# A top-k attention and MLP kernel: the mask from the k-th score minus the scores, weights decoded through PSUM, and a planner that takes transposes in turn

## The chip, the cores and the metric

The kernel runs on 1 core of one Trainium2 chip. The metric is the device time of one launch in microseconds (us), the median over repeated runs; lower is better. Engines are named as in the profile: PE (TensorE matmul, PEld its weight loads), DVE (VectorE), ACT (ScalarE), POOL (GpSimd), SP (SyncE, which here issues the DMAs).

## The reference

Top-k attention over 4 batches, 8 heads, 576 positions and head size 64, then two MLPs on the 2304 tokens of width 512 with a hidden width of 2048. The weights arrive as float64 and are read as pairs of 32-bit words.

```python
scores = (1 / sqrt(64)) * q @ k.T                    # per head, 576 x 576
kth    = np.partition(scores, -32)[..., -32:-31]     # 32nd largest of each row
scores = np.where(scores >= kth, scores, -1e9)
attn   = softmax(scores)
x      = (attn @ v)  as tokens x 512
h = x @ w_in;   g = h if h >= 1, 0 if h <= -1, else (h + 1)**2 / 4;   x = g @ w_out
h = max(x @ w_in2, 0);   out = (h * h) @ w_out2
```

## The kernel before

**Work.** A slot is one 128-row score tile of one head: 144 slots, eight to a token tile T. For each slot PE writes 576 scores into a PSUM area (there are two areas, used in turn). DVE then finds the 32 largest of each row with four MAX8 and three MATCH_REPLACE8, which take the first scores from PSUM and go on in an SBUF tile W. POOL makes two one-column numbers from the maxima (`exp_bias`, tile nb), ACT masks with a Prelu that reads the scores once more (`below`) and so is the last reader of the PSUM area, ACT takes the exponential (`exp`), ACT and POOL split it into a high and a low half (tile pc), SP issues a DMA transpose (pT), and PE multiplies by v (`attend`). Every token tile then has four groups in each MLP: 12 matmuls into a tile h, ACT and DVE work on it (`mlp_act`, `mlp_gate`), a split on ACT and POOL (tile g), a DMA transpose (gT), and 12 matmuls into o.

**Weights.** All four weight matrices end in one SBUF tile, wall. A chunk (64 of them, two of them in halves) is loaded as float64 words, decoded to fp32 by `w_decode` on ACT, POOL and DVE, measured on PE (`w_norm`, tiles gram), and once its whole matrix is decoded scaled and split into two fp16 halves (`w_split`; for 24 chunks the low half goes PE to ACT through PSUM tiles lo_i and lo_o). The decodes run during about the first 230 us, among the first slots.

**Order.** `Book.order` is a planner: it gives each operation a cost (`Book.costs`), a key (its step, eight steps to a slot, less a shift for urgent kinds) and its dependencies, and runs all five engines' lists forward in planned time. The order that comes out is the order in which each engine's queue is written; on the chip an engine works through its queue in order and waits on semaphores. The planner keeps operations of different engines apart that hold the same "bank": a PSUM tile, or "port", which every POOL operation holds and every DVE operation with two SBUF inputs.

**Buffers.** PSUM pool `ps_h` has two buffers under one tag "h", given out in rotation: the h tiles of the MLP groups, the lo tiles of `w_split` and the small tiles of `global_scale` share it. An allocation waits until the last but one has been released. The maxima (m8) have three buffers, nb and W four each.

```python
        if engine == "POOL" or engine == "DVE" and sum(not v.tile.ring.psum for v in ins if v.elements() > 64) > 1:
            op.banks.add("port")
    ...
    dch=(0, 1, 3)          # steps of the three parts of a decode
    scores=-6, bias=7, below=8, exp=9, phi=10
```

Of the kernel before, what the change touches and what calls it, by code (L numbers as in the profile page):

```python
# [8 lines left out]
F32 = mybir.dt.float32  # L9
# [7 lines left out]
P = 128  # L17
# [130 lines left out]
class Book:  # L148
# [36 lines left out]
    def note(self, engine, method, fn, args, kwargs):  # L185
        op = Op()
        op.n, op.engine, op.fn, op.args, op.kwargs = len(self.ops), engine, fn, args, kwargs
        views = [a for a in (*args, *kwargs.values()) if isinstance(a, View)]
        outs = [a for a in (*args[:1], kwargs.get("out"), kwargs.get("accum_out")) if isinstance(a, View)]
        ins = [a for a in views if not any(a is o for o in outs)]  # L190
        if method == "matmul" and not kwargs["start"]:
            ins.append(args[0])
        deps = set(self.hold)
        op.tiles, op.new = [], []
        for v in views:
            t = v.tile
            if t not in op.tiles:
                op.tiles.append(t)
                t.left += 1
                if t.first is None:  # L200
                    t.first = op.n
                    op.new.append(t)
                else:
                    deps.add(t.first)
        for v in ins:
            c = v.cover()
            before = [n for d, n in v.tile.writes if meet(c, d)]
            assert before, (method, v.tile.name)
            deps.update(before)
            v.tile.reads.append((c, op.n))  # L210
        for v in outs:
            c = v.cover()
            t = v.tile
            for kind in (t.writes, t.reads):
                kept = []
                for d, n in kind:
                    if n == op.n:
                        kept.append((d, n))
                        continue
                    if meet(c, d):  # L220
                        deps.add(n)
                        if not c[4] and c[0] <= d[0] and c[1] >= d[1] and c[2] <= d[2] and c[3] >= d[3]:
                            continue
                    kept.append((d, n))
                kind[:] = kept
            t.writes.append((c, op.n))

        op.opens = op.closes = []
        if method == "matmul":
            p0, p1, at = outs[0].cover()[:3]  # L230
            parts = [(outs[0].tile, at // 2048, p) for p in range(p0 // 64, (p1 + 63) // 64)]
            op.opens = parts if kwargs["start"] else []
            op.closes = parts if kwargs["stop"] else []
        op.load = method == "dma_start"
        op.move = method
        if op.load:
            if self.beat:
                deps.add(self.beat[-1])
        elif len(self.beat) > WINDOW:
            deps.add(self.beat[-WINDOW])  # L240
        if engine == "DVE" and method == "max":
            self.beat.append(op.n)
        deps.discard(op.n)
        op.deps = deps
        op.banks = {v.tile for v in views if v.tile.ring.psum}
        if engine == "POOL" or engine == "DVE" and sum(not v.tile.ring.psum for v in ins if v.elements() > 64) > 1:
            op.banks.add("port")
        op.cost = self.costs(engine, method, args, kwargs, outs, ins)
        op.key = (self.step + self.shift, op.n)
        self.ops.append(op)  # L250


    def costs(self, engine, method, args, kwargs, outs, ins):
# [7 lines left out]
        if method == "dma_start_transpose":  # L261
            return (1.33 if n < 1100 else 1.41), n * 256 / 1000 / 165
        if method == "dma_start":
            return 0.6, 4 * (n or args[1].elements()) * 128 / 1000 / 400
        if engine == "DVE":
            if method == "max":
                return 0.68, 0.75
# [7 lines left out]
        if method == "memset":  # L275
            return 0.07, 0.07
        c = 0.14 + n / 522 if method == "tensor_tensor" else 0.14 + n / 940 + (0.08 * aps if n < 8 else 0.0)
        return c, c


    def order(self):
# [35 lines left out]
        while len(out) < len(ops):  # L317
# [29 lines left out]
            if op.closes:  # L347
# [1 line left out]
                for s in shut:  # L349
                    heapq.heappush(soon[s.engine], (t, s.n))  # L350
                shut.clear()
            for b in op.banks:
                held.setdefault(b, {})[e] = t + took + 0.08
            free[e] = t + busy
            if op.load:
                wire = max(wire, t + 1.6) + took
                end = wire + 0.7
            elif op.move == "dma_start_transpose":
                wire = max(wire, t + 1.1) + took
                end = wire + 0.4  # L360
            else:
                end = t + took
            out.append(op)
            for n in op.succ:
                s = ops[n]
# [30 lines left out]
def tile_topk_attention_mlp_mlp(  # L396
# [111 lines left out]
    def w_decode(name, c, *half):  # L508
        d = wall[:, W[name]["at"] + c + 1, :].bitcast(I32)
        if half:  # L510
            d = d[:, 256 * half[0] : 256 * half[0] + 256]
        words = lambda: raw[(name, c, *half)].rearrange("p (n w) -> p n w", w=2)
        halves = lambda: raw[(name, c, *half)].bitcast(U16).rearrange("p (n w) -> p n w", w=4)
        hi = lambda: words()[:, :, 1]


        low = lambda: halves()[:, :, 1]
        return [
            lambda: ACT.activation(hi(), hi(), AF.Prelu, scale=2.0**-112, alpha=-(2.0**32)),
            lambda: POOL.tensor_scalar(d, low(), 2.0**-13, 2.0**-14 - 0.5, op0=ALU.mult, op1=ALU.add),  # L520
            lambda: DVE.scalar_tensor_tensor(d, hi().bitcast(I32), 3, d, op0=ALU.logical_shift_left, op1=ALU.bitwise_or),
        ]

    gram = {}
# [252 lines left out]
    def q_scale(T):  # L777
        n2 = small.tile([P, 1], F32, tag="qn2", name=f"qn2_{T}")
        sq = small.tile([P, 2], F32, tag="sq", name=f"sq_{T}")
        esc = small.tile([P, 2], F32, tag="esc", name=f"esc_{T}", bufs=3)  # L780

        ld["sq", T] = sq

# [7 lines left out]
        def exp_scale():  # L791
            for half in range(2):
# [1 line left out]
                POOL.tensor_scalar(  # L794
                    esc[:, half : half + 1], isk[:, b : b + 1], sq[:, 1:2], 0.125, op0=ALU.mult, op1=ALU.mult
                )
            POOL.tensor_scalar(esc, esc, 2.0**-56, 1.0, op0=ALU.max, op1=ALU.mult)
            ld["esc", T] = esc

        return (  # L800
# [6 lines left out]
    def q_prep(T, half):  # L807
# [21 lines left out]
        def trans():  # L829
# [2 lines left out]
                out=qt.rearrange("p a h t -> p (a h) t"), in_=hl().rearrange("p a h b d -> p (a h b d)")  # L832
            )
            for jj in range(4):
                st[8 * T + 4 * half + jj] = dict(qt=qt[:, :, jj, :], esc=ld["esc", T][:, half : half + 1])

        return [split_hi, split_lo, copy_lo, trans]

# [38 lines left out]

    def exp_bias(t):
        d = st[t]
        nb = small.tile([P, 2], F32, tag="nb", name=f"nb_{t}", bufs=4)  # L880
        last = d["m"][:, TOPK - 1 : TOPK]
        d["nb"] = nb
        if t in PLAN["md"]:
            POOL.tensor_scalar(nb[:, 1:2], d["m"][:, 0:1], d["esc"], -1.0, op0=ALU.mult, op1=ALU.mult)
            return
        POOL.tensor_scalar(nb[:, 0:1], last, -1.0, 1.0, op0=ALU.mult, op1=ALU.mult)
        POOL.tensor_scalar(nb[:, 1:2], last, d["m"][:, 0:1], d["esc"], op0=ALU.subtract, op1=ALU.mult)

    def below(t):
        d = st[t]  # L890
        if t in PLAN["md"]:
            return
        ACT.activation(d["e"], d["s"], AF.Prelu, bias=d["nb"][:, 0:1], scale=1.0, alpha=2.0**97)

    def exp(t):
        d = st[t]
        by = t in PLAN["md"]
        ACT.activation(d["e"], d["s"] if by else d["e"], AF.Exp, bias=d["nb"][:, 1:2], scale=d["esc"])
        if by:
            DVE.scalar_tensor_tensor(d["e"], d["s"], d["m"][:, TOPK - 1 : TOPK], d["e"], op0=ALU.is_ge, op1=ALU.mult)  # L900

# [510 lines left out]
```

## Time and profile before

| | us |
|---|---|
| median of 3 runs (lowest, highest) | 1121.82 (1120.46, 1122.23) |
| profiled execution, its own time | 1122.3 |
| its span in the profile | 1120.4 |
| PE busy in the span | 986.2 (88%) |
| DVE busy | 918.2 (82%) |
| ACT busy | 868.2 (77%) |
| POOL busy | 719.0 (64%) |

The span is what the trace covers; 1.9 us of the execution's own time lie outside it. A busy share is a mean over stages: in the first quarter of the span weights are loaded and decoded among the first slots, the middle holds slots and MLP groups, and the last 110 us or so hold MLP groups alone.

### The profile page before, as it was taken

The page shows a single profiled execution, that of the slowest core. Times are in us where ns is not written, and L with a number is a line of the kernel's source. Part 1 is how long each engine was busy: PE and PEld are TensorE (multiplying, and loading weights), DVE is VectorE, ACT ScalarE, POOL GpSimd, SP SyncE. Part 2 cuts the span into 40 slices and gives each one's busy share as a digit, 9 for nine tenths or more (in the row PEclk, how much of TensorE's full clock was granted, in tenths as well). Part 3 has the DMA queues.
Part 4 walks back from the last instruction along what each step waited for, and adds up shares of the span by engine and source line. Part 5 has one row for each costly group of instructions (what it writes and reads, how often), then busy time and mean ns, then how long its engine had stood idle before and what let it go on. Part 6 is the DMA issues. An engine that isn't in the chain of part 4 may idle for free.

```text
span 1120.4 us, 20689 instructions
## 1 busy us (share of the span) xinstructions
PE 986.2 (88%) x6676; PEld 478.3 (43%) x6676; DVE 918.2 (82%) x1992; ACT 868.2 (77%) x1605; POOL 719.0 (64%) x1182
## 2 busy tenths in 40 slices
PE   1258577777999999999999999999999999999997
PEld 0034333333444444454444444444444444444443
DVE  3988888798999999999899999999899999992100
ACT  4568879998987777888888888988788778776532
POOL 4596989979786756557776646567685646454221
PEclk9999888789999999999999999999999999999999
DMA  7996887686897766878988687879867676654332
GB/s 205 305 311 177 239 230 160 139 178 116 145 168 147 132 117 118 157 133 155 170 145 147 109 128 128 159 136 172 156 123 129 114 133 99 120 109 99 71 61 56
DMA packets 463389, 165.21 MB, mean 147 GB/s; under 512 B 441777, under 2 KB 448945, under 8 KB 463281
## 3 DMA queue, kind: packets, MB, share of 16 engines
q1 hardware_dynamic: 459856, 163.05, 71.5%
q10 hardware_dynamic: 3424, 0.85, 0.5%
q8 instruction: 52, 0.85, 0.3%
q14 instruction: 57, 0.46, 0.1%
HBM read 55.31 MB, written 4.72 MB: 54 GB/s over the span
## 4 chain that ended last, share of the span: by engine, by line
PE 31%; POOL 15%; issue 10%; ACT 9%; DMA 9%; DVE 9%; SPq 1%; POOLq 0%; ACTq 0%; DVEq 0%
PE o L383 14%; PE h L383 12%; DMA gT<-g 5%; POOL pc L383 4%; DVE m L383 4%; PE s L383 4%; DVE W L383 3%; POOL g L383 3%; POOL wall L383 3%; ACT r L383 2%; ACT W L383 2%; POOL nb L383 2%; SPq L383 1%; DMA l_q<-in_q_dram 1%; ACT g L383 1%
## 5 line engine op out<-in xcount | busy, mean ns | idle before, releaser
L383 PE MATMUL o<-wall,gT 128*128 128x512 f16 x1728 | 427.7, 383 | 18.6 <-DMA gT<-g 17.1
L383 DVE MAX8 m<-W 128x8 f32<-128x576 f32 x432 | 326.0, 756 | 7.1
L383 POOL TENSOR_TENSOR g<-r,g 128x512 f16<-128x512 f32 x144 | 167.0, 1160 | 173.0 <-ACT g L383 157.6
L383 PEld LDWEIGHTS <-gT 128*128 128x128 f16 x1728 | 164.1, 98 | 226.6 <-DMA gT<-g 41.8
L383 POOL TENSOR_TENSOR pc<-W,pc 128x64 f16<-128x64 f32 (+1 forms) x288 | 208.9, 745 | 68.3 <-ACT pc L383 63.7
L383 DVE MATCH_REPLACE8 W<-m,W 128x576 f32<-128x576 f32 x288 | 213.8, 743 | 0.0
L383 PE MATMUL h<-wall,T_x 128*128 128x512 f16 x864 | 209.7, 384 | 1.7 <-DVE r L383 1.1
L383 PE MATMUL h<-wall,T_y 128*128 128x512 f16 x864 | 207.3, 379 | 0.2 <-ACT r L383 0.2
L383 ACT ACTIVATE W<-s,nb 128x576 f32<-128x576 f32 x144 | 106.0, 736 | 46.4 <-POOL nb L383 39.8
L383 DVE MAX8 m<-s 128x8 f32<-128x576 f32 x144 | 109.5, 760 | 37.9 <-PE s L383 25.8
L383 PE MATMUL s<-kst,qT 128*128 128x64 f16 (+3 forms) x640 | 102.0, 300 | 35.9 <-ACT W L383 33.0
L383 ACT ACTIVATE W<-W,nb,esc 128x576 f32<-128x576 f32 x144 | 124.6, 865 | 11.1 <-POOL nb L383 5.1
L383 PEld LDWEIGHTS <-T_x 128*128 128x128 f16 x864 | 81.6, 99 | 94.4 <-issue 7.8
L383 PEld LDWEIGHTS <-T_y 128*128 128x128 f16 x864 | 81.3, 98 | 91.2 <-issue 0.7
L383 PEld LDWEIGHTS <-pT 128*128 128x128 f16 (+1 forms) x2240 | 90.8, 102 | 60.8 <-issue 17.6
L383 PE MATMUL s<-vst,pT 128*128 128x65 f16 (+1 forms) x2240 | 98.9, 196 | 13.9 <-DMA pT<-pc 9.5
L383 DVE MATCH_REPLACE8 W<-m,s 128x576 f32<-128x576 f32 x144 | 107.6, 748 | 0.0
L383 ACT ACTIVATE pc<-W 128x576 f16<-128x576 f32 x144 | 97.3, 676 | 1.2
L383 ACT ACTIVATE g<-r 128x512 f16<-128x512 f32 x144 | 89.8, 624 | 8.8 <-DVE r L383 7.4
L383 ACT ACTIVATE r<-r 128x512 f32<-128x512 f32 x144 | 90.5, 629 | 2.8
L383 ACT ACTIVATE r<-h 128x512 f32<-128x512 f32 x72 | 42.5, 590 | 62.7 <-PE h L383 61.3
L383 ACT ACTIVATE r<-h,B,A 128x512 f32<-128x512 f32 x72 | 55.8, 775 | 42.1 <-PE h L383 41.3
(143 smaller groups left out, 1101.0 us busy)
## 6 DMA issues: line engine op xcount, KB each, us to landing
wall<-in_moe_w_in_dram SPq DMA_DIRECT2D x32, 512.0 KB, 7.6
wall<-in_moe_w_out_dram SPq DMA_DIRECT2D x30, 512.0 KB, 5.3
out_dram<-ob SPq DMA_DIRECT2D x18, 256.0 KB, 2.6
l_q<-in_q_dram SPq DMA_DIRECT2D x16, 256.0 KB, 3.5
n_v<-in_v_dram SPq DMA_DIRECT2D x24, 144.0 KB, 2.8
n_k<-in_k_dram SPq DMA_DIRECT2D x12, 288.0 KB, 3.2
l_k<-in_k_dram SPq DMA_DIRECT2D x12, 288.0 KB, 3.3
pT<-pc SPq DMA_TRANSPOSE x144, 3.4
```

The source lines that it names most:

```text
L383: op.fn(*(real(a) for a in op.args), **{k: real(a) for k, a in op.kwargs.items()})
```

## The change

It has three parts. **Mask**: `below` computes Prelu(kth - s), with the 32nd maximum itself as its bias and a scale of -1; a slope of 2^-97 on the side of the kept scores is taken back by `exp`, whose scale is now -(2^97) times the old one (two more columns of tile esc, clamped so that the product stays finite, made by one more POOL operation per token tile). `exp_bias` is left with one POOL operation instead of two. **Decode**: the three parts of a decode come in the order POOL, ACT, DVE instead of ACT, POOL, DVE; ACT writes the decoded high words to a tile of the "h" ring in PSUM instead of back over the raw words in SBUF, the planner lets that operation start only behind the POOL part, and the DVE operation takes one input from PSUM, so that it no longer holds the "port" bank. **Planner**: DMA transposes hold a bank "turn", which keeps those of SP's queue and of ACT's queue apart until the data have landed; a plain load costs 0.1 us more on the wire and counts at half the rate where its target has three or more dimensions; a POOL operation that reads 16-bit words costs 0.1 us more.

```diff
@@ note
+        if method == "dma_start_transpose":
+            op.banks.add("turn")
@@ costs
         if method == "dma_start":
-            return 0.6, 4 * (n or args[1].elements()) * 128 / 1000 / 400
+            n = n or args[1].elements()
+            return 0.6, 0.1 + 4 * n * 128 / 1000 / (200 if outs and len(outs[0].ap.ap) > 2 else 400)
...
+        if any(v.ap.dtype is U16 for v in ins):
+            c += 0.1
         return c, c
@@ order
-            for b in op.banks:
-                held.setdefault(b, {})[e] = t + took + 0.08
...
+            for b in op.banks:
+                held.setdefault(b, {})[e] = end + 0.08
@@ w_decode
         low = lambda: halves()[:, :, 1]
+        ps = []
+
+        def bits():
+            POOL.tensor_scalar(d, low(), 2.0**-13, 2.0**-14 - 0.5, op0=ALU.mult, op1=ALU.add)
+            ps.append(len(book.ops) - 1)
+
+        def top():
+            ps.append(ps_h.tile([P, 4, P], F32, tag="h", name=f"dec_{name}_{c}").rearrange("p a b -> p (a b)")[:, 0 : 256 if half else 512])
+            book.hold = ps[:1]
+            ACT.activation(ps[1], hi(), AF.Prelu, scale=2.0**-112, alpha=-(2.0**32))
+            book.hold = ()
+
         return [
-            lambda: ACT.activation(hi(), hi(), AF.Prelu, scale=2.0**-112, alpha=-(2.0**32)),
-            lambda: POOL.tensor_scalar(d, low(), 2.0**-13, 2.0**-14 - 0.5, op0=ALU.mult, op1=ALU.add),
-            lambda: DVE.scalar_tensor_tensor(d, hi().bitcast(I32), 3, d, op0=ALU.logical_shift_left, op1=ALU.bitwise_or),
+            bits,
+            top,
+            lambda: DVE.scalar_tensor_tensor(d, ps[1].bitcast(I32), 3, d, op0=ALU.logical_shift_left, op1=ALU.bitwise_or),
         ]
@@ q_scale
-            POOL.tensor_scalar(esc, esc, 2.0**-56, 1.0, op0=ALU.max, op1=ALU.mult)
+            POOL.tensor_scalar(esc[:, 0:2], esc[:, 0:2], 2.0**30, 2.0**-56, op0=ALU.min, op1=ALU.max)
+            POOL.tensor_scalar(esc[:, 2:4], esc[:, 0:2], -(2.0**97), 1.0, op0=ALU.mult, op1=ALU.mult)
@@ exp_bias
-        POOL.tensor_scalar(nb[:, 0:1], last, -1.0, 1.0, op0=ALU.mult, op1=ALU.mult)
-        POOL.tensor_scalar(nb[:, 1:2], last, d["m"][:, 0:1], d["esc"], op0=ALU.subtract, op1=ALU.mult)
+        POOL.tensor_scalar(nb, last, d["m"][:, 0:1], d["esc"], op0=ALU.subtract, op1=ALU.mult)
@@ below
-        ACT.activation(d["e"], d["s"], AF.Prelu, bias=d["nb"][:, 0:1], scale=1.0, alpha=2.0**97)
+        ACT.activation(d["e"], d["s"], AF.Prelu, bias=d["m"][:, TOPK - 1 : TOPK], scale=-1.0, alpha=2.0**-97)
@@ exp
-        ACT.activation(d["e"], d["s"] if by else d["e"], AF.Exp, bias=d["nb"][:, 1:2], scale=d["esc"])
+        ACT.activation(d["e"], d["s"] if by else d["e"], AF.Exp, bias=d["nb"], scale=d["esc"] if by else d["nsc"])
```

## Rows read from the trace of the kernel before

**Rows 1.** Windows: PE, PEld, DVE, ACT, POOL busy; PE clock, DMA share, GB/s.

```profile
28.00:84.00 56.00, 20.55 (x122) 11.36 (x123) 48.74 (x107) 34.92 (x64) 41.69 (x70) 1.00 1.00 308
84.00:224.00 140.00, 101.20 (x671) 49.50 (x669) 116.57 (x250) 122.13 (x242) 119.32 (x158) 0.87 0.76 189
224.00:280.00 56.00, 43.52 (x292) 21.22 (x293) 49.85 (x116) 51.35 (x112) 47.88 (x70) 0.91 0.74 147
280.00:1008.00 728.00, 710.32 (x5040) 346.06 (x5039) 679.54 (x1472) 595.23 (x1075) 467.95 (x828) 1.00 0.75 137
1008.00:1120.00 112.00, 105.56 (x527) 47.50 (x525) 12.31 (x29) 51.04 (x89) 28.95 (x33) 0.98 0.36 72
```

**Rows 2.** Waits, 28 to 224 us: us in total, times, longest us.

```profile
PE s L383 <- ACT W L383: 31.6, 14, 8.1
ACT W L383 <- POOL nb L383: 23.2, 13, 8.4
DVE m L383 <- PE s L383: 8.5, 5, 5.4
```

**Rows 3.** Timeline, 139.5 to 147 us: start, us, engine [idle before, releaser].

```profile
139.83 0.75 DVE L383 MAX8 m<-W 128x8 f32<-128x576 f32 x1
...
142.93 0.19 POOL L383 TENSOR_SCALAR nb<-m 128x1 f32<-128x1 f32 x1
...
143.15 0.74 ACT L383 ACTIVATE W<-s,nb 128x576 f32<-128x576 f32 x1 [3.70 <-POOL nb L383]
...
143.94 1.12 PE L383 MATMUL s<-kst,qT 128*128 128x64 f16 x4 [3.37 <-ACT W L383]
```

**Rows 4.** DVE groups by form, 28 to 224 us: count | busy us, mean ns.

```profile
L383 DVE SCALAR_TENSOR_TENSOR wall<-wall 128x512 int32<-128x512 int32 x57 | 45.7, 802 | 13.1 <-POOL wall L383 7.1 <-ACT wall L383 5.5 <-issue 0.5
...
L383 DVE MAX8 m<-s 128x8 f32<-128x576 f32 x22 | 16.7, 758 | 11.1 <-PE s L383 8.5 <-ACT wall L383 1.7 <-ACT qhl L383 0.8
...
L383 DVE SCALAR_TENSOR_TENSOR r<-h,G,r 128x512 f32<-128x512 f32 x5 | 3.7, 739 | 0.1
```

**Rows 5.** Instructions of tile wall: ns min/median/max, first and last start us.

```profile
L383 POOL TENSOR_SCALAR wall<-wall x62: 640/655/1184, 10.2 to 209.5; 128x512 int32<-128x512 uint16 x62
L383 DVE SCALAR_TENSOR_TENSOR wall<-wall x62: 660/692/1480, 10.9 to 211.0; 128x512 int32<-128x512 int32 x62
```

**Rows 6.** POOL groups by form, 28 to 224 us.

```profile
L383 POOL TENSOR_SCALAR wall<-wall 128x512 int32<-128x512 uint16 x56 | 42.6, 760 | 12.5 <-DMA wall<-in_moe_w_in_dram 7.8 <-DMA wall<-in_moe_w_out_dram 0.7
...
L383 POOL TENSOR_SCALAR nb<-m,esc 128x1 f32<-128x1 f32 x21 | 11.2, 534 | 0.4
...
L383 POOL TENSOR_SCALAR nb<-m 128x1 f32<-128x1 f32 x21 | 6.4, 306 | 14.9 <-DVE m L383 13.8
```

**Rows 7.** POOL groups by form, 300 to 1000 us.

```profile
L383 POOL TENSOR_SCALAR nb<-m,esc 128x1 f32<-128x1 f32 x110 | 40.3, 367 | 0.0
```

**Rows 8.** ACT groups by form, 84 to 224 us.

```profile
L383 ACT ACTIVATE wall<-wall 128x512 f32<-128x512 f32 x33 | 21.5, 671 | 0.5 <-DMA wall<-in_moe_w_out_dram 0.5
...
L383 ACT ACTIVATE h<-h,NG,A 128x512 f32<-128x512 f32 x5 | 3.7, 743 | 0.0
```

**Rows 9.** Waits of SP's queue, whole span.

```profile
SPq L383 <- DMA kst<-wall: 19.3, 2, 14.1
```

**Rows 10.** Timeline of ACT, 8 to 60 us.

```profile
26.27 0.42 ACT L383 ACTIVATE qhl<-l_q 128x256 f16<-128x256 f32 x1 [6.33 <-issue]
```

**Rows 11.** Windows of 28 us inside 280 to 1008 us, two of 26.

```profile
476.00:504.00 28.00, 28.00 (x200) 14.02 (x199) 26.43 (x63) 23.98 (x44) 15.54 (x25) 1.00 0.71 133
532.00:560.00 28.00, 26.18 (x190) 12.93 (x189) 24.61 (x52) 24.15 (x46) 20.57 (x36) 1.00 0.98 170
```

**Rows 12.** Timeline, 125 to 147 us: the first h tile and the next lo tile.

```profile
125.73 2.39 PE L383 MATMUL h<-wall,T_x 128*128 128x512 f16 x8
...
144.33 0.73 DVE L383 SCALAR_TENSOR_TENSOR r<-h,G,r 128x512 f32<-128x512 f32 x1
...
146.27 1.15 PE L383 MATMUL lo_o<-wall 128*128 128x512 f32 x1
```

More of the change, by code (lines that the diff above doesn't have):

```diff
@@ L779, in q_scale @@
         sq = small.tile([P, 2], F32, tag="sq", name=f"sq_{T}")
-        esc = small.tile([P, 2], F32, tag="esc", name=f"esc_{T}", bufs=3)
+        esc = small.tile([P, 4], F32, tag="esc", name=f"esc_{T}", bufs=3)
         ld["sq", T] = sq
@@ L834, in trans @@
             for jj in range(4):
-                st[8 * T + 4 * half + jj] = dict(qt=qt[:, :, jj, :], esc=ld["esc", T][:, half : half + 1])
+                st[8 * T + 4 * half + jj] = dict(qt=qt[:, :, jj, :], esc=ld["esc", T][:, half : half + 1], nsc=ld["esc", T][:, half + 2 : half + 3])
         return [split_hi, split_lo, copy_lo, trans]
@@ L879, in exp_bias @@
         d = st[t]
-        nb = small.tile([P, 2], F32, tag="nb", name=f"nb_{t}", bufs=4)
+        nb = small.tile([P, 1], F32, tag="nb", name=f"nb_{t}", bufs=4)
         last = d["m"][:, TOPK - 1 : TOPK]
@@ L883, in exp_bias @@
         if t in PLAN["md"]:
-            POOL.tensor_scalar(nb[:, 1:2], d["m"][:, 0:1], d["esc"], -1.0, op0=ALU.mult, op1=ALU.mult)
+            POOL.tensor_scalar(nb, d["m"][:, 0:1], d["esc"], -1.0, op0=ALU.mult, op1=ALU.mult)
             return
-        POOL.tensor_scalar(nb[:, 0:1], last, -1.0, 1.0, op0=ALU.mult, op1=ALU.mult)
-        POOL.tensor_scalar(nb[:, 1:2], last, d["m"][:, 0:1], d["esc"], op0=ALU.subtract, op1=ALU.mult)
+        POOL.tensor_scalar(nb, last, d["m"][:, 0:1], d["esc"], op0=ALU.subtract, op1=ALU.mult)
     def below(t):
```

## The prediction

> **What bounds the kernel now.** I read the windows first, to find the stages. From 280 to 1008 us PE is busy 710.32 of 728 us at full clock, and behind 1008 us it works on alone, 105.56 of 112 us, with DVE done [rows 1]. There the time is PE's own work, and no other engine can take more off than PE's 17.7 us and 6.4 us of idling. Before 280 us it is otherwise: in 84 to 224 us PE has 101.20 of 140 us, its granted clock averages 0.87 of full, and ACT, POOL and DVE stand at 122.13, 119.32 and 116.57 us, none of them full [rows 1]. That is a stage of three nearly loaded engines that wait on each other. In 28 to 84 us the DMA share is 1.00 at 308 GB/s: the weights come as fast as they can, and faster engines gain little there [rows 1]. All slots and groups follow in one order, so what the first stage gains arrives at the end nearly whole, because from 280 us on PE always has the next group to do.
>
> Then the waits of 28 to 224 us, where the slots themselves are held up. They form a chain: ACT's mask waits for POOL's nb (23.2 us, 13 times), PE's next scores wait for the mask, which is the last reader of the score area (31.6 us, 14 times), and DVE's first MAX8 waits for these scores (8.5 us, 5 times) [rows 2]. The totals are not to be added: they are the same delay seen from three engines, and only what reaches DVE slows the top-k search. One case in the timeline: DVE has the last maximum at 139.83 + 0.75 = 140.58 us, but POOL's queue is in other work and makes nb at 142.93; ACT, idle for 3.70 us, starts the mask at 143.15, and PE, idle for 3.37 us, the scores at 143.94 [rows 3].
>
> Last, the forms of one operation beside each other. DVE's part of a decode has a mean of 802 ns in this stage but a median of 692 and a maximum of 1480; POOL's part a mean of 760, a median of 655, a maximum of 1184 [rows 4 to 6]. POOL's second nb operation takes 534 ns on average here and 367 ns later, when no weights are decoded [rows 6, 7]. The same instruction on the same shape is stretched only while DVE's decode, with two inputs from SBUF, runs against POOL. DVE's gate on the h tile, one input from PSUM, has a mean of 739 ns in the same stage and the stretch is not seen [rows 4].
>
> **The decode, DVE.** The new DVE operation has one input in PSUM and one in SBUF like the gate. Its price lies between the decode's fastest, 660 ns, and today's mean of 802 (no gain) [rows 4, 5]; I take the gate's 739, the nearest row. 57 x (802 - 739) = 3.6 us come off DVE; the bounds are 0 and 57 x (802 - 660) = 8.1 us. [...]
>
> **POOL.** If the stretching goes, 56 decodes save 760 - 655 = 105 ns each, 5.9 us, and the remaining nb saves 21 x 167 ns = 3.5 us; the nb that is dropped saves 21 x 306 ns = 6.4 us [rows 5 to 7]. Against that stand three or so additional esc operations, at most 0.4 us each by the one-column nb, 1 us. So POOL is about 15 us lighter in 28 to 224 us. It is not the engine that ends each wait, and a good part only turns into idling: I count 2 us, with bounds of 0 and, if POOL set the pace, 15.
>
> **ACT, and the order of the parts.** ACT's part of a decode costs 671 ns now; the only ACT row that writes PSUM is the h pass with its two pointer operands, 743 ns [rows 8]. No row says how SBUF to PSUM compares, so the bounds are 72 ns dearer (2.4 us over 33) and as much cheaper; I take no change. ACT is now behind POOL instead of beside it, so a chunk that DVE stands waiting for comes up to one ACT pass, 0.67 us, later. DVE waits for POOL's and ACT's parts 7.1 and 5.5 us now [rows 4]; I let the longer chain eat what a quicker POOL would give back there, zero.
>
> **The mask.** The Prelu then waits for DVE alone. Of the case above 143.15 - 140.58, some 2.5 us, would go; the exponential behind it still needs nb, so ACT's wait moves one instruction on, with the splits and decodes of ACT's queue behind it, but the score area is free and PE and DVE go on. What reaches DVE today is 8.5 us [rows 2, 4]; not all of these waits begin at POOL, so I take half, 4.3 us; bounds 0 and 8.5. The maxima are now held until ACT has read them; with three buffers and the mask starting before nb did, I cost that at nothing, and if that cover were gone a MAX8 would wait one mask longer.
>
> From 280 us on the same edits take one short operation per slot off POOL, which has 467.95 of 728 us, and shorten a chain that PE is not waiting for [rows 1]. I count nothing there.
>
> **The planner.** On the chip SP's queue already waits for the landing of the other queue's transposes, 19.3 us in all, and ACT stands still for 6.33 us on the same account at 26.27 us [rows 9, 10]. The planner's turn does not add that wait, it only lets the queues be filled with it in mind. Bounds: nothing, and the 6.33 us if all of ACT's standstill were in the way; the loads are what that stage waits for, so I take 1 us. The costs of loads and of 16-bit POOL work move planned times by fractions of a microsecond: nothing on the mean. But every queue is written anew, also in the middle, where 28 us windows differ from 28.00 to 26.18 us of PE work [rows 11]. If all 26 windows were like the worst the stretch would idle 47 us instead of 17.7; if all were like the best, none. An order drawn again rarely goes far to either side, and I keep 4 us each way for it in the range.
>
> **The shared ring.** Each decode now takes a tile of the two-buffer "h" ring from ACT's pass to the end of DVE's, some 0.67 + 0.74 = 1.4 us plus a queue's delay. The first h tile shows what rotation costs: it is taken at 125.73 us and its gate ends at 144.33 + 0.73 = 145.06, and the next-but-one tile, a lo tile, starts only at 146.27 [rows 12]. During such a life a single decode gets through. PE is idle 38.8 of 140 us in that stage [rows 1] and takes up most of it; eight groups fall in the time of the decodes, and I charge one decode's hold for one group in six or so, 2 us. Bounds are in the rival below.
>
> **Sum.** -3.6 (DVE decode) - 2 (POOL) - 4.3 (mask) - 1 (turn) + 2 (ring) = -8.9 us on the profiled execution's own 1122.3 us, which is 1.9 us above its span and 0.5 us above the median: 1113.4 there, and 1113 as a median.
>
> **Rivals.** *Hidden.* The first stage is held by the loads (DMA share 1.00 to 84 us, 0.76 after it) or by ACT, the busiest engine of 84 to 224 us, whose work does not shrink; the turn changes nothing, since the chip waits already. Then the relief becomes idling of POOL and DVE: 1120 to 1124 us. For it: ACT's 122.13 us. Against: ACT itself idles on nb in the same stage.
>
> *Slower by the ring.* Decodes, lo tiles and h tiles queue for two buffers. If each of the eight groups costs the decodes behind it two holds of 1.4 us, and one hold more as it asks for its own tile behind them, that is 8 x 3 x 1.4 = 34 us of waiting; at PE's busy share of 0.72 about 24 us reach the end, less the 11 us gained: 1122 + 13 = 1135 us. It decides from 11 us of ring waits on the path, an added 1.4 us per group. For it: the 19 us life of the first h tile. Against: that life was long because DVE had decodes to do before the gate, and blocked decodes bring the gate forward.
>
> *Slower by the order.* The new order leaves PE idle more often from 280 us on. At 0.65 us more in each of 26 windows that is 17 us, and 1122 - 9 + 17 = 1130 us. For it: windows of 26.18 us exist. Against: no edit lengthens a chain of that stretch.
>
> *All the relief arrives.* DVE 8.1, mask 8.5, POOL 6, turn 1, with no ring cost: 1122 - 24 = 1098 us.
>
> **Numbers.** A change under 0.2% (2.2 us) cannot be told from none with this kernel. Forecast case (1104 to 1119 us) 0.62, all relief 0.05, hidden 0.14, ring 0.12, order 0.07. Faster by over 0.2% takes the first two, 0.67; same is the hidden case, 0.14; slower the last two, 0.19. The range reaches over the hidden case and the milder half of the slower ones: 1102 to 1126 us.
>
> **What would show it.** In the profile after: DVE's decode near 739 ns with no instruction far above it, POOL's near 655, the nb row near 367 in the first stage too. The wait of the mask for POOL's nb gone and PE's wait for the mask well under 31.6 us; the exponential's wait for nb is what is late next. The first-stage windows reach the same slot about 8 us earlier, and PE's busy time from 280 us on stays near 97.6%. The prediction is wrong if waits for h-ring tiles turn up at ACT's decode pass or before PE's first h matmul, if the stretch from the same slot to the end changes by more than 4 us, or if the decode on DVE is dearer than 802 ns.

## The result

| | median us | lowest to highest | ratio to the kernel before, 95% interval |
|---|---|---|---|
| before | 1122.03 | 1120.46 to 1124.27 | 1 |
| after | 1105.1 | 1104.7 to 1107.98 | 0.9838 [0.9819, 0.9857] |

The change takes 16.9 us off by the medians, 18 by the ratio. Forecast were 8.9 off and a time of 1113 us. The sign and the range (1102 to 1126) hold; the size is half of what came. The profiled execution took 1105.2 us with a span of 1103.4.

**Where the time went.** The span is PE's busy time plus its idle time. The windows of after (PE, PEld, DVE, ACT, POOL busy; PE clock, DMA share, GB/s), the stages those of [rows 1]:

```profile
28.00:84.00 56.00, 22.92 (x140) 12.24 (x140) 50.01 (x116) 37.78 (x69) 36.47 (x70) 0.57 0.94 293
84.00:224.00 140.00, 104.98 (x749) 52.61 (x750) 122.21 (x268) 132.69 (x269) 110.00 (x154) 0.90 0.85 208
224.00:280.00 56.00, 49.85 (x319) 23.04 (x318) 47.91 (x115) 54.79 (x118) 47.54 (x64) 0.97 0.68 142
280.00:1008.00 728.00, 710.69 (x5023) 345.77 (x5022) 664.21 (x1443) 585.36 (x1059) 447.27 (x719) 1.00 0.74 136
1008.00:1104.00 96.00, 88.22 (x419) 39.36 (x416) 6.10 (x16) 38.48 (x66) 22.17 (x24) 1.00 0.32 64
```

Up to 280 us PE idled 109.7 us before and 97.2 after, 12.4 less (280 less the busy time of the four windows from 0 on: 170.3 and 182.8). From 280 to 1008 us it idled 17.7 and 17.3, behind 1008 us 6.9 and 7.2. Its busy time fell from 986.2 to 981.7 for the same matmuls, and the granted clock rose where most of the early ones run: 0.87 became 0.90 in 84 to 224 us, 0.91 became 0.97 in the next window (means over stretches at 1.00 and at 0.50; h's 128x512 matmul takes 634 ns by the median in 204 to 212 us of after, at 0.50, and 379 from 280 to 1008 us, at 1.00). The 0.57 of 28 to 84 us, 1.00 before, speaks the other way; PE has only 22.9 us of work there, and three other orders of the same kernel, told of below, show 0.88, 1.00 and 0.88. Together -12.4 - 0.4 + 0.3 - 4.5 = -17.0, the difference of the spans. So all of the gain is made before 280 us, and it shows as the work that is left behind 1008 us: 105.6 us before, 88.2 after.

**The waits.** The rows of after that answer to [rows 2], 28 to 224 us, in us, times and longest us:

```profile
PE s L388 <- ACT W L388: 19.7, 6, 8.0
ACT W L388 <- DVE m L388: 17.9, 5, 8.4
DVE m L388 <- PE s L388: 5.5, 7, 1.2
ACT W L388 <- POOL nb L388: 3.6, 4, 1.4
```

ACT's 23.2 us behind POOL's nb became 17.9 us behind the maxima themselves, and 3.6 us behind nb, which is now the exponential's wait. Much of both is the start, where ACT waits for slots that are still being searched: one wait of 8.4 us before, two of 8.4 and 6.3 after. From 44 us on, ACT waits 14.8 us before and 3.2 + 3.6 after, and PE's wait for the mask is nearly gone (44 to 224 us, before and then after):

```profile
PE s L383 <- ACT W L383: 23.1, 12, 4.1
```

```profile
PE s L388 <- ACT W L388: 4.1, 2, 3.8
```

DVE's wait for scores, 28 to 224 us, went from 8.5 us with a longest of 5.4 to 5.5 with a longest of 1.2. The timeline of one slot in after (start, us, engine [idle before, releaser]), to be held against [rows 3]:

```profile
129.72 0.73 ACT L388 ACTIVATE W<-s,m 128x576 f32<-128x576 f32 x1
...
130.51 0.65 PE L388 MATMUL s<-kst,qT 128*128 128x64 f16 x4 [0.26 <-ACT W L388]
...
130.77 0.37 POOL L388 TENSOR_SCALAR nb<-m,esc 128x1 f32<-128x1 f32 x1
...
131.52 0.86 ACT L388 ACTIVATE W<-W,nb,esc 128x576 f32<-128x576 f32 x1
```

The mask runs 1.05 us ahead of nb, PE starts the next scores before nb exists, and ACT has a decode and a split to do before the exponential.

**The decode.** Groups by form of after, 28 to 224 us, DVE and then POOL (count | busy us, mean ns | idle before, releasers):

```profile
L388 DVE SCALAR_TENSOR_TENSOR wall<-dec_o,wall 128x512 int32<-128x512 int32 x30 | 20.4, 685 | 10.4 <-ACT dec_o L388 9.7 <-POOL wall L388 0.4
L388 DVE SCALAR_TENSOR_TENSOR wall<-dec_i,wall 128x512 int32<-128x512 int32 x26 | 17.4, 681 | 2.3 <-issue 1.0 <-ACT dec_i L388 0.7 <-POOL pc L388 0.3
...
L388 POOL TENSOR_SCALAR wall<-wall 128x512 int32<-128x512 uint16 x56 | 37.3, 666 | 11.6 <-DMA wall<-in_moe_w_in_dram 6.0 <-DMA wall<-in_moe_w_out_dram 1.3
L388 POOL TENSOR_SCALAR nb<-m,esc 128x1 f32<-128x1 f32 x25 | 9.2, 369 | 18.6 <-DVE m L388 17.2 <-DMA n_v<-in_v_dram 1.0
```

DVE's part fell from 802 to 681 and 685 ns, POOL's from 760 to 666, the remaining nb from 534 to 369 [rows 4, 6]. No DVE decode is stretched any more, and hardly a POOL one; minimum, median and maximum of after, beside [rows 5]:

```profile
L388 POOL TENSOR_SCALAR wall<-wall x62: 638/656/1105, 10.4 to 209.9; 128x512 int32<-128x512 uint16 x62
L388 DVE SCALAR_TENSOR_TENSOR wall<-dec_i,wall x32: 659/681/692, 13.7 to 147.2; 128x512 int32<-128x512 int32 x32
L388 DVE SCALAR_TENSOR_TENSOR wall<-dec_o,wall x34: 407/684/692, 69.3 to 230.5; 128x512 int32<-128x512 int32 x30, 128x256 int32<-128x256 int32 x4
```

DVE's maximum was 1480 ns and is 692. It is not that the two engines no longer meet: 56 of the 62 full DVE decodes of after overlap a POOL instruction. Of POOL's 62, 19 took over 720 ns before, 16 of them beside DVE's decode and 3 beside another DVE operation with two tiles from SBUF, and 3 do now, and each of these 3 overlaps a DVE operation that still reads two tiles from SBUF (into vst, or of wall with sk). In nine kernels of this document with the decode in PSUM no full DVE decode is above 693 ns; without it, 22 of the 62 of before are above 720, with a maximum of 1480, and the maxima of the three orders of mask and planner are 1630 to 1651. DVE's waits for the other parts of a decode are a little less, 7.1 + 5.5 us before, and now 9.7 + 0.7 behind ACT and 0.4 behind POOL. ACT's own part, into PSUM, in 84 to 224 us [rows 8]:

```profile
L388 ACT ACTIVATE dec_o<-wall 128x512 f32<-128x512 f32 x21 | 13.3, 634 | 1.0 <-DVE wall L388 1.0
L388 ACT ACTIVATE dec_i<-wall 128x512 f32<-128x512 f32 x16 | 10.0, 635 | 0.0
```

**Ring and planner.** ACT's waits for a buffer of the "h" ring, 8 to 300 us (its decode pass waits until an earlier tile's reader is through):

```profile
ACT dec_o L388 <- DVE wall L388: 1.0, 3, 0.5
ACT dec_i L388 <- DVE wall L388: 0.6, 2, 0.3
ACT dec_o L388 <- DVE r L388: 0.2, 1, 0.2
```

That is 1.8 us at ACT. PE waits at the ring's lo tiles too, in the same window:

```profile
PE lo_o L388 <- DVE r L388: 3.2, 1, 3.2
PE lo_i L388 <- DVE wall L388: 2.9, 4, 1.4
PE lo_o L388 <- DVE wall L388: 2.6, 2, 2.0
```

A lo tile takes nothing from the gate (tile r), so the 3.2 us are the ring's; the 5.5 us behind DVE's writes to wall can be the ring's or those of the tile's own inputs. Before, PE's waits of these kinds came to 0.7 us. That makes 5.0 to 10.5 us of ring waits, where the ring rival needed 11 on the path; PE idles 35.0 us in 84 to 224 us with them and 38.8 before.

SP's wait for the other queue's transposes went from 19.3 to 13.5 us. ACT's standstill of 6.33 us behind its second kst transpose is gone [rows 9, 10]; the only one of its kind left in 8 to 300 us is 1.48 us behind its first transpose, of qT. After, the waits of SP's queue and the timeline of ACT:

```profile
SPq L388 <- DMA kst<-wall: 13.5, 2, 12.2
```

```profile
12.27 0.78 ACT L388 ACTIVATE wall<-wall,sk 128x576 f16<-128x576 f32 x1 [1.48 <-issue]
```

### The profile page after: what moved, and what is told of

It reads as the page before. It is cut to its first block, busy times and chain, and to the rows that moved or that the text cites. A ratio compares the mean times of both kernels' runs of the same rounds, so it can differ in the third digit from the quotient of the medians.

```text
span 1103.4 us, 20579 instructions
## 1 busy us (share of the span) xinstructions
PE 981.7 (89%) x6676; PEld 476.0 (43%) x6676; DVE 905.7 (82%) x1992; ACT 862.3 (78%) x1605; POOL 674.0 (61%) x1056
## 4 chain that ended last, share of the span: by engine, by line
PE 43%; DVE 15%; ACT 14%; DMA 12%; issue 7%; POOL 6%; SPq 1%; POOLq 0%; ACTq 0%; DVEq 0%
PE o L388 19%; PE h L388 17%; DMA gT<-g 7%; PE s L388 6%; DVE m L388 6%; DVE W L388 5%; ACT W L388 3%; ACT wall L388 2%; ACT r L388 2%; POOL g L388 2%; POOL pc L388 2%; DVE wall L388 2%; ACT pc L388 1%; DMA qT<-qhl 1%; SPq L388 1%
## 5 line engine op out<-in xcount | busy, mean ns | idle before, releaser
L388 POOL TENSOR_TENSOR pc<-W,pc 128x64 f16<-128x64 f32 (+1 forms) x288 | 205.3, 734 | 56.9 <-ACT pc L388 52.0
L388 ACT ACTIVATE W<-s,m 128x576 f32<-128x576 f32 x144 | 105.9, 736 | 43.6 <-DVE m L388 34.0
L388 ACT ACTIVATE W<-W,nb,esc 128x576 f32<-128x576 f32 x144 | 124.7, 867 | 16.9 <-POOL nb L388 12.2
L388 PE MATMUL s<-kst,qT 128*128 128x512 f16 (+3 forms) x640 | 102.7, 298 | 23.6 <-ACT W L388 21.7
L388 POOL TENSOR_SCALAR nb<-m,esc 128x1 f32<-128x1 f32 x144 | 53.3, 370 | 103.7 <-DVE m L388 90.1
```

Source lines behind the costliest of these rows:

```text
L388: op.fn(*(real(a) for a in op.args), **{k: real(a) for k, a in op.kwargs.items()})
```

## The experiments

All kernels here compute the whole reference. The theories by their letters, as the expectations use them. A: each part relieves the first stage and the parts add up. B: the decode carries it all. C: the planner's costs carry it. D: the gain is mostly the luck of one order of the queues; D2: the change is worth some 9 us and its own order was lucky; A2: it is worth 17 and the first redrawn order was unlucky; E: the kernel before had a lucky order. F, G and H belong to the last runs and are told in their expectations.

### One part at a time

Each kernel is the kernel before with some of the hunks of the change.

```diff
@@ decode_alone: the hunk of w_decode
+            ACT.activation(ps[1], hi(), AF.Prelu, scale=2.0**-112, alpha=-(2.0**32))
...
+            lambda: DVE.scalar_tensor_tensor(d, ps[1].bitcast(I32), 3, d, op0=ALU.logical_shift_left, op1=ALU.bitwise_or),
@@ mask_alone: the hunks of q_scale, exp_bias, below, exp
+        ACT.activation(d["e"], d["s"], AF.Prelu, bias=d["m"][:, TOPK - 1 : TOPK], scale=-1.0, alpha=2.0**-97)
@@ planner_alone: the hunks of note, costs, order
+            op.banks.add("turn")
@@ no_decode: all but the hunk of w_decode
```

> The kernel before with the decode part alone (POOL, ACT into PSUM, DVE with one PSUM input). Theory A: 6 to 10 us faster, about 1114. Theory B: 13 to 18 us faster, about 1106. Theory C: within 2 us of before.

> The kernel before with the mask part alone (Prelu on kth minus s, bias from the maxima, one nb operation less). Theory A, that every part relieves the three loaded engines of the first stage and the parts add up: 4 to 7 us faster than before, about 1116, with the wait of ACT for nb before 224 us nearly gone. Theory B, that the decode through PSUM carries it all: within 2 us of before. Theory C, that the planner's corrected costs carry it: within 2 us of before.

> The kernel before with the planner part alone (transposes in turn, dearer loads and 16-bit POOL operations); no instruction of the program changes, only the order in the queues. Theory A: 1 to 4 us faster, about 1119. Theory B: within 2 us of before. Theory C: 10 us faster or more, under 1112.

> The changed kernel with the decode part undone (mask and planner stay). Theory A: 1111 to 1115 us, the mask's and the planner's share of the gain. Theory B: within 3 us of before, 1119 or more. Theory C: within 3 us of the changed kernel, 1108 or less.

Measured: decode alone 0.9944 [0.9924, 0.9963], mask alone 1.0014 [0.9998, 1.0029], planner alone 0.9978 [0.9960, 0.9996], mask and planner without the decode 1.0091 [1.0060, 1.0122]. The three parts alone multiply to 0.9936; all three together give 0.9838. A fails as a sum, B and C fail: no part alone brings half of it. By themselves the decode (6 us) and the planner (2.5 us) lie in A's ranges and the mask does not; the pair without the decode, 10 us slower, lies in nobody's. In mask alone the wait by which the prediction sized the mask is down from 8.5 us to a quarter, 28 to 224 us, and the time is not less:

```profile
DVE m L383 <- PE s L383: 2.2, 3, 0.8
```

What decode alone looks like is the more telling: its search for the maxima of slot 24 (the first MAX8) starts 17.3 us ahead, at 220.9 us against 238.2 in before, that of slot 40 only 1.9 us ahead. Its PE waits of 224 to 340 us show two that before does not have, and in its window of 252 to 280 us PE is less busy than in before (22.03 us), after more in the window ahead of it (26.10 us of 28, 21.49 in before):

```profile
PE o L383 <- POOL wall L383: 3.6, 4, 1.4
PE o L383 <- ACT wall L383: 3.4, 2, 3.1
```

```profile
252.00:280.00 28.00, 21.42 (x125) 9.19 (x124) 20.89 (x55) 27.96 (x59) 25.34 (x37) 0.88 0.55 116
```

PE has the slots, but the last weights of w_out2 are not split yet. The last four half chunks of that matrix (tile w_o), ACT's pass in before, in decode alone and in after (ns min/median/max, first to last start):

```profile
L383 ACT ACTIVATE w_o<-w_o x4: 416/426/437, 205.1 to 222.9; 128x256 f32<-128x256 f32 x4
```

```profile
L383 ACT ACTIVATE dec_o<-w_o x4: 385/390/395, 232.1 to 248.4; 128x256 f32<-128x256 f32 x4
```

```profile
L388 ACT ACTIVATE dec_o<-w_o x4: 384/406/412, 214.5 to 229.7; 128x256 f32<-128x256 f32 x4
```

Decode alone decodes its last half chunk 25.5 us later than before; after only 6.8 us later, and its waits of that kind are 1.2 us in all. A lead of the slots is worth what the weights behind them allow.

### The order kept

An order written by the planner was kept and only the emitted operations exchanged. `later` replaces what the last planned operation emits.

```diff
@@ same_order_old_mask: the kernel after, in its own order, emits the mask of before
+        later(lambda: d["one"]() or nc.scalar.activation(d["e"].real(), d["s"].real(), AF.Prelu, bias=d["nb2"][:, 0:1], scale=1.0, alpha=2.0**97))
@@ old_order_new_mask: the kernel before, in its own order, emits the new mask
+        later(lambda: None)
...
+        later(lambda: nc.scalar.activation(d["e"].real(), d["s"].real(), AF.Prelu, bias=d["m"][:, TOPK - 1 : TOPK].real(), scale=-1.0, alpha=2.0**-97))
```

> The changed kernel with its order of all queues kept, but with the old mask put into these places: Prelu waits for a negated maximum that POOL makes (written into POOL's queue where Prelu starts, so 144 more POOL operations of one column), old signs and scales; the extra esc operation stays. Theory A, that each part is worth something by itself in a given order: 3 to 7 us slower than the changed kernel, 1108 to 1112. Theory D, that most of the gain is the order that came out (a draw) and the mask's waits are hidden: within 2 us of the changed kernel.

> The kernel before with its order of all queues kept, but with the new mask in these places: the negating POOL operation is left out, Prelu takes the maxima as its bias; one esc operation more per token tile. Theory A: 3 to 6 us faster than before, since the wait of ACT for nb falls away in the same order. Theory D: within 2 us of before.

Measured: 0.9992 [0.9972, 1.0012] with the old mask in the order of after, some 17 us slower than after; 0.9989 [0.9968, 1.0010] with the new mask in the order of before. The waits of 28 to 224 us, of the first kernel and of the second:

```profile
ACT W L930 <- POOL nb L915: 26.3, 14, 8.7
PE s L388 <- ACT W L930: 26.1, 11, 8.2
```

```profile
PE s L383 <- ACT W L910: 21.3, 11, 7.8
ACT W L917 <- POOL nb L383: 9.7, 7, 2.7
ACT W L910 <- DVE m L383: 8.5, 2, 8.2
```

In the order of before the new mask (L910) no longer waits for nb; 8.5 us behind the maxima stay, 8.2 of them at the first slot, and 9.7 us behind nb turn up at the exponential (L917). PE's wait for the mask falls from 31.6 to 21.3 us, DVE's for scores only from 8.5 to 7.7, and the time by 1.2 us with an uncertainty of 2.4. That is what D forecast, and not A. The reverse run fits neither (A 3 to 7 us, D within 2), and it is not clean: it puts 144 more POOL operations into queues that were not planned for them, so its 17 us is not the price of the wait.

### The order drawn again

A planning cost is nudged by 0.2 to 0.7%. No operation changes; the queues are written in another order.

```diff
@@ before_draw1, after_draw1
-            c = max(n * (4 if args[2].ap.dtype is F32 else 1) / 2370.0, 0.03)
+            c = max(n * (4 if args[2].ap.dtype is F32 else 1) / 2375.0, 0.03)
@@ before_draw2, after_draw2
-            c = 0.155 + n / 1400 - (0.03 if wide else 0.0) + 0.09 * aps - (0.04 if n < 300 else 0.0)
+            c = 0.156 + n / 1400 - (0.03 if wide else 0.0) + 0.09 * aps - (0.04 if n < 300 else 0.0)
@@ before_draw4, after_draw4
-                return 0.76, 0.85
+                return 0.765, 0.85
```

> The kernel before with one cost of the planner moved by 0.2% (2375 in place of 2370 columns per us of PE), nothing else: another draw of the order. Theory A: within 3 us of before. Theory D: orders differ by 5 us or more without any cause in the program, so this one may lie anywhere from 1110 to 1135, and mask alone, planner alone and no decode tell of draws, not of parts.

> The changed kernel with the same planner cost moved by 0.2%. Theory A: within 3 us of the changed kernel. Theory D: 5 to 15 us slower than the changed kernel, the changed kernel being a lucky draw.

> The changed kernel with the planner's fixed cost of an ACT operation at 0.156 in place of 0.155 us: another draw of its order. Theory D2, that the change is worth about 9 us and its own order is a lucky draw: 1109 to 1118 us. Theory A2, that the change is worth 17 us and draw 1 was an unlucky order: 1108 us or less.

> The changed kernel with the planner's cost of MATCH_REPLACE8 at 0.765 in place of 0.76 us: another draw. Theory D2: 1109 to 1118 us. Theory A2: 1108 us or less.

> The kernel before with the planner's fixed cost of an ACT operation at 0.156 in place of 0.155 us. Theory D2: before's orders spread too, 1118 to 1128 us around a mean near the kernel before. Theory E, that before itself was the lucky draw of its kind: 1126 us or more.

> The kernel before with the planner's cost of MATCH_REPLACE8 at 0.765 in place of 0.76 us. Theory D2: 1118 to 1128 us. Theory E: 1126 us or more.

| order | before | after |
|---|---|---|
| own | 1 | 0.9838 [0.9819, 0.9857] |
| draw 1 | 1.0021 [1.0001, 1.0041] | 0.9931 [0.9904, 0.9957] |
| draw 2 | 0.9976 [0.9954, 0.9998] | 0.9869 [0.9828, 0.9911] |
| draw 4 | 1.0111 [1.0082, 1.0141] | 0.9891 [0.9865, 0.9917] |
| mean | 1.0027 | 0.9882 |

Every order of after is faster than every order of before. The means differ by 0.0145, 16 us (about 0.006 to 0.023 from the scatter of four and four). So D falls as an account of the whole: the gain is there without the luck of one order. Its forecast for draw 1 of after did come (5 to 15 us slower, measured 10), and A's (within 3 us) did not. By their own times the two later orders of after, 1110.4 and 1111.8 us, lie in D2's range and not in A2's; of before's, 1121.6 us lies in D2's and 1135.3 us in E's. D2 is right in part: the own order of after lies 0.0044, 5 us, below the mean of its kind, and 10 us below draw 1; E likewise, with 3 us. D2's 9 us is too little and A2's size is right on average, though draw 1 is no more out of the way than the own order. One nudge of before costs 12 us, and its windows show where:

```profile
224.00:280.00 56.00, 39.34 (x245) 18.73 (x246) 45.70 (x107) 49.59 (x110) 46.89 (x67) 0.82 0.68 132
280.00:1008.00 728.00, 708.09 (x4987) 343.69 (x4986) 666.26 (x1457) 586.42 (x1067) 463.61 (x821) 1.00 0.75 136
1008.00:1134.00 126.00, 118.58 (x632) 54.41 (x628) 26.21 (x56) 62.13 (x105) 37.01 (x49) 0.99 0.38 75
```

Against [rows 1] it has 4.2 us less PE busy time in 224 to 280 us, at a clock of 0.82, idles 2.2 us more from 280 to 1008 us, and has 13 us more left behind it. With a scatter like this, a part's own order alone cannot say what a part is worth, the runs above included.

### The parts over several orders

Decode alone and mask with planner, each with the second and fourth nudge, and decode with planner (all but the mask) in its own order and with the second.

```diff
@@ decode_draw2, no_decode_draw2, no_mask_draw2: as draw 2
@@ decode_draw4, no_decode_draw4: as draw 4
@@ no_mask: the kernel after with the hunks of q_scale, exp_bias, below and exp taken back
-        ACT.activation(d["e"], d["s"], AF.Prelu, bias=d["m"][:, TOPK - 1 : TOPK], scale=-1.0, alpha=2.0**-97)
+        ACT.activation(d["e"], d["s"], AF.Prelu, bias=d["nb"][:, 0:1], scale=1.0, alpha=2.0**97)
```

> Decode alone, planned with ACT's fixed cost at 0.156 instead of 0.155. Four orders of the kernel before have a mean ratio of 1.003, four of the kernel after 0.988; decode alone in its own order gave 0.994. Theory F (the decode carries nearly all of the mean gain, whatever the order): this run and its sister with the match_replace cost have a mean of 0.988 to 0.992 with the run before. Theory G (the parts share it): a mean of 0.995 to 0.999. Theory H (no part is worth anything without the others): 1.000 to 1.006.

> Decode alone, planned with MATCH_REPLACE8 at 0.765 instead of 0.76, the nudge that took the kernel before to 1.011 and the kernel after to 0.989. F: well under 1.000, about 0.990, and the DVE decode near 683 ns as in every order with the decode. G: 0.995 to 1.003. H: 1.003 or more. All three: the DVE decode and POOL's part without stretched instructions.

> Mask and planner without the decode, planned with ACT's fixed cost at 0.156. In its own order this pair gave 1.009. F: the three orders of the pair have a mean like that of the kernel before, 1.000 to 1.006. G: their mean is 0.993 to 0.999, so this run would have to come out near 0.990. H: 1.000 to 1.006, as with F; the two are told apart by decode alone.

> Mask and planner without the decode, planned with MATCH_REPLACE8 at 0.765. F and H: between 0.998 and 1.011, the spread of the orders of the kernel before. G: 0.988 to 0.997.

> Decode and planner, with the old mask (two POOL operations for nb, ACT's mask behind POOL). F (the decode carries nearly all): 0.985 to 0.993. G (the parts share it): 0.992 to 0.997. H (only all together): 0.998 to 1.006. All: ACT's wait for POOL's nb in 28 to 224 us is back at 20 us or more, the DVE decode near 683 ns.

> Decode and planner with the old mask, planned with ACT's fixed cost at 0.156. Read with its sister as a mean of two orders. F: the mean is 0.985 to 0.993. G: 0.992 to 0.997. H: 0.998 to 1.006.

| order | before | decode alone | mask + planner | decode + planner | all |
|---|---|---|---|---|---|
| own | 1 | 0.9944 [0.9924, 0.9963] | 1.0091 [1.0060, 1.0122] | 0.9947 [0.9931, 0.9963] | 0.9838 |
| draw 2 | 0.9976 | 0.9936 [0.9917, 0.9955] | 1.0048 [1.0031, 1.0066] | 1.0013 [0.9997, 1.0029] | 0.9869 |
| draw 4 | 1.0111 | 1.0009 [0.9993, 1.0025] | 1.0068 [1.0043, 1.0092] | | 0.9891 |
| PE busy up to 280 us, mean | 168.3 | 173.8 | 168.6 | 175.7 | 181.7 |
| PE busy from 280 us on, mean | 821.4 | 812.9 | 820.7 | 814.2 | 801.3 |

The last row is the work that is left at a granted clock of 0.98 or more. It is the better measure of the two: up to 280 us PE is also busy longer where its clock is lower (634 ns a matmul at 0.50 against 379 at 1.00 in after, as above).

Read along the rows, the decode alone gains 0.0056, 0.0040 and 0.0102, on average 7 us. Added to mask and planner it gains 0.0253, 0.0179 and 0.0177, 23 us. The mask added to decode and planner gains 0.0109 and 0.0144, 14 us; mask and planner without the decode lose 0.0091 and 0.0072 and gain 0.0043. The planner added to the decode does nothing (+0.0003) or loses (+0.0077). Step by step, decode, planner and mask thus gain 5, -4 and 14 us on average of these two orders, 15 in all. How sure is this? The orders of one kind scatter by 0.0044 about their mean (all five kinds, draw 1 included), which leaves a gain over three rows uncertain by about 0.008 and one over two rows by about 0.010. The decode's 0.0066 alone is not clear of that, its 0.0203 beside mask and planner is, and the mask's 0.0127 beside decode and planner is only just.

So F falls (decode alone was to be at 0.988 to 0.992, its two redrawn orders have a mean of 0.997, which is in G's range), G falls (mask and planner were to gain by themselves), and H is right for the mask and wrong for the decode. Decode and planner have a mean of 0.998, in H's range, with ACT's wait for nb back at 19.8 and 20.6 us as forecast. What the rows agree on: each gains by the decode, and more beside the other parts than alone; the mask gains in both orders beside the decode, and by itself neither of its two runs (1.0014 and, in the kept order, 0.9989) moves clear of the noise.

Why the mask needs the decode, the traces of the two pairs suggest, and no run isolates it. Without the decode part, ACT's two passes over W in 28 to 224 us, and DVE's decode and POOL's nb in the same kernel (mask and planner, own order):

```profile
L388 ACT ACTIVATE W<-W,nb,esc 128x576 f32<-128x576 f32 x22 | 19.0, 862 | 7.8 <-POOL nb L388 7.6
L388 ACT ACTIVATE W<-s,m 128x576 f32<-128x576 f32 x22 | 16.1, 730 | 20.3 <-DVE m L388 16.9 <-DVE sv L388 2.5 <-DVE sc_q L388 0.8
...
L388 DVE SCALAR_TENSOR_TENSOR wall<-wall 128x512 int32<-128x512 int32 x56 | 46.3, 830 | 13.8 <-POOL wall L388 12.0 <-POOL pc L388 1.5 <-issue 0.3
...
L388 POOL TENSOR_SCALAR nb<-m,esc 128x1 f32<-128x1 f32 x22 | 12.1, 552 | 22.3 <-DVE m L388 19.2 <-DVE rs L388 2.3 <-DVE sc_q L388 0.2
```

The exponential waits 7.6 us for an nb that is still stretched (552 ns; 3.6 us and 369 ns in after), and DVE's decode runs into POOL rather more than in before: 830 ns here and 878 in the second order of this pair, 802 in before. But that second order is faster than the own (1.0048 against 1.0091), so this length alone does not set the time. Without the mask but with the decode, the last half chunk is late: ACT's pass over it starts at 237.0 to 248.4 us in the five orders of that kind, and PE waits 0.4 to 7.0 us, on average 5, for the split of its matrix in 224 to 340 us; with both, the pass starts at 227.8 to 235.4 us and the waits are 0 to 4.5, on average 1.4. That could account for some 4 of the mask's 14 us there.

## Why the prediction was right and wrong

**Right.** The stage: all of the gain is made before 280 us, and from there on PE idles as it did (17.3 and 17.7 us, 97.6% busy; over four orders each 18.4 and 17.7). The stretching ends with the second SBUF input: POOL's decode at 666 ns and its nb at 369 against 655 and 367 forecast. The mask's wait for nb goes and the exponential's is next. ACT as the last part but one costs DVE nothing on balance. The hidden, the ring and the slower order rivals did not come.

**Wrong: the sum of parts, above all the mask's term.** The prediction took -3.6 - 2 for the decode and -4.3 for the mask, as reliefs that stand side by side. The decode alone measures 7 us over three orders, with some 9 us of uncertainty; -5.6 was near. The mask was sized by half of the 8.5 us that DVE waited in before [rows 2], "not all of these waits begin at POOL". The trace tells which do: of the five waits, two follow a mask that stood waiting for nb, 0.8 us at the first slot (37.96 us) and 0.3 us at 123.53. The longest follows a mask that ACT started without idling, late because its queue was in other work (before; start, us, engine [idle before, releaser]):

```profile
207.71 0.72 ACT L383 ACTIVATE W<-s,nb 128x576 f32<-128x576 f32 x1
...
208.49 0.98 PE L383 MATMUL s<-kst,qT 128*128 128x64 f16 x4 [3.00 <-ACT W L383]
...
210.35 0.77 DVE L383 MAX8 m<-s 128x8 f32<-128x576 f32 x1 [5.38 <-PE s L383]
```

So by its own reasoning the term was 1 us, and measured by itself the mask is worth that or nothing: 0.9989 in the order of before, 1.0014 alone. Beside decode and planner it is worth 12 and 16 us, by a way that the prediction does not have. The step that failed is to price each part by a wait and to add the prices: the wait of a stage in which three engines hold each other was taken for the price of one of them. That the delay only moves to the next wait while POOL and DVE still collide, and is freed once they do not, fits the kept order, where 9.7 us turned up at the exponential; it is a reading of the traces, and no run isolates it.

**Mis-sized beside it.** DVE's decode measures 683 ns and not 739: 57 x (802 - 683) = 6.8 us instead of 3.6. The gate was the wrong nearest row: it has a pointer operand and fp32 arithmetic, the decode has neither, and no run tells which of the two makes the 56 ns between them. With the PSUM input the decode takes 681 to 685 ns, no more than the median of 692 with two inputs from SBUF [rows 5]. The ring's waits are 5.0 to 10.5 us where 2 were charged; what they cost in time no run isolates. The planner's 1 us is 2.5 us in planner alone, inside the scatter of the orders, and a loss beside the decode (0 and 9 us). The search of slot 0 begins 3.3 us earlier in after, at 20.3 us, but that is the planner's only in part: 1.5 us in planner alone, 2.8 in decode alone. Two slips changed no forecast: the all-relief rival takes 6 us for POOL where the bound was 15, which would give 1089 us, and the least busy window of the middle is not the 26.18 us of [rows 11] but one of 25.68, at 336 to 364 us.

**Wrong: 4 us for the order.** Orders of one kernel spread over 0.9976 to 1.0111 (15 us) before and 0.9838 to 0.9931 (10 us) after. The mean of four orders of after is 0.9882 of 1122 us, 1108.8 us. So of the 8 us between 1113 and 1105, half is the sum, 1113 to 1108.8, and half is the place of the own order among its kind, 1108.8 to 1105. Put the other way, the 18 us are 16 of mean gain and 5 of luck in the order of after, less 3 of luck in the order of before.

**Wrong: that what the slots gain arrives nearly whole.** The first stage reaches the same slot 17 to 23 us earlier (slots 16 and 24), not 8. Of that, 21.6 us at slot 40 became 17.0 at the end: the stretch behind it is 4.6 us longer, more than the 4 that the prediction had set as a sign of being wrong. Its other sign, ring waits at ACT's decode pass, showed too, with 1.8 us. In decode alone 17.3 us at slot 24 became 1.9 at slot 40. What arrives is PE work done, and that needs the weights as much as the slots.

**Open.** Some 10 of the mask's 14 us beside the decode have no wait to their name, and why the last half chunks come earlier with the new mask was not tried by itself.

## What to carry to other kernels

In a stage where several engines wait on each other, the wait of one is no price: remove it alone and it may turn up elsewhere at the same cost (here 9.7 us at the exponential), so size a change by the PE work that is left behind a fixed time and expect parts to depend on each other. Where queues are written by a planner, nudge one of its costs by half a per cent a few times on both sides before a difference under 1% is put down to the edit. A lead of one stream of work is worth only as much as the latest of the other streams that the same engine needs (in decode alone 17.3 us became 1.9).

## What the runs showed of the hardware

A DVE scalar_tensor_tensor of 512 int32 per partition with one input from PSUM took 681 to 685 ns, no more than the median of 692 ns with two SBUF inputs, one of which was read at every second word [rows 5]; the gate, fp32 with one input from PSUM and a pointer operand, took 739 [rows 4]. ACT's decode from SBUF to PSUM took 634 ns against 671 in place in SBUF [rows 8], where it also wrote every second word; the two differences were not tried apart. In before, each of POOL's 19 full decodes above 720 ns and each of the 7 of its 144 second nb operations above 400 ns overlapped a DVE operation with two tiles from SBUF, and each of DVE's 22 full decodes above 720 ns overlapped a POOL operation. DVE's maximum fell from 1480 to 692 ns when one of its inputs came from PSUM, though 56 of 62 instructions still overlapped POOL's, and POOL's mean fell from 760 to 666. Two tiles are not the only case: dg_k, a DVE tensor_scalar with one 128x128 bf16 tile from SBUF, took 236 to 254 ns three times in before, apart from POOL, and 1409 ns beside POOL operations at 252.77 us.
